# Batch 0 of a fused attention and maxout kernel: DMA work reordered, score pairs ended earlier, more filler matmuls

## The chip, the cores and the metric

The kernel runs on one core of a Trainium2 chip. The metric is the device time of one execution in microseconds (us), and the figure given is the median of several runs. A core has TensorE (PE in the profile; PEld is its loading of weights), VectorE (DVE), ScalarE (ACT) and GpSimd (POOL). SP does no arithmetic: here it issues DMA transfers, and so does POOL. Each of them works through its own list of instructions in order and waits for the others through semaphores. Matmuls write to PSUM, a small memory of eight banks for each partition; everything else lies in SBUF.

## The reference

```python
# attention without softmax: batch 8, seq S = 3072, width D = 256, d_qk = 64
scores = (1 / S) * z @ z.T              # per batch, 3072 x 3072, symmetric
attn   = np.maximum(scores, 0) ** 2
x      = u * (attn @ v)                 # then flattened to 24576 tokens x 256
# maxout layer: d_ff = 1024
h1 = x @ w1
h2 = x @ w2
out = np.maximum(h1, h2) @ w_out        # 24576 x 256, float32
```

The scores are symmetric, so a block of them below the diagonal is the transpose of one above it. The maximum is rewritten as max(h1, h2) = relu(x (w1 - w2)) + x w2, so that the second layer is relu(x w15) w_out + x W2o with w15 = w1 - w2 and W2o = w2 w_out, which are made once on the chip.

## The kernel before

**Tiles and groups.** A batch has 24 tiles of 128 positions. A group is four query tiles (512 positions); six groups make a batch and 48 the whole, in the order of the list `groups`, whose index is i. A group and a key tile are written (g, n) below, of batch 0 unless another is named, and a block (g, blk) is the four key tiles of `blk` against the queries of group g.

**Scores.** `score_pair` (line 125) takes two key tiles against the group's 512 queries: two matmuls (line 134) into two PSUM banks, a Relu of each into `r_sb` (line 149 on ScalarE, or line 145 on VectorE where `dve_half` says so), and one VectorE multiply (line 153) that squares both into `a_sb`. Two pairs fill a block. Only blocks on and above the diagonal are computed, 42 pairs in a batch. Of a block above it, SP issues a DMA transpose (line 157) that makes the mirrored block `at_sb`, which a later group reads. `a_sb` blocks rotate through ten buffers (`apool`), mirrored blocks through thirteen (`tpool`), and the first three loads of z, w1, w2 and w2T take buffers of that same `tpool`: the eleventh mirrored block gets the buffer of w1, the twelfth that of w2, and the thirteenth that of w2T, once these have been read.

**Attention.** `attn_unit` (line 164) does one key tile: four matmuls (line 175) of 64 rows by 512 columns, into the accumulators acc0 and acc1. These take four banks and exist once, so the next group can start only when `drain` (line 179) has emptied them: two ScalarE copies (line 183) and two VectorE adds (line 186). `gate` (line 189) multiplies the sum by u into `xT`; `ff1` (line 202) and `ff2` (line 220) are the maxout layer. From the third group on (i = 2) `ff1` of an earlier group stands between a group's last key tile and the next group's first, so that TensorE has work while the accumulators drain. i = 2 does two of them. The other four PSUM banks (`mm_psum`) rotate among scores, z transposes, `ff1` and `ff2`.

**The order by hand.** The schedule is written out in the main loop (lines 314 to 396); nothing reorders it. `ahead(k)` (line 264) emits score pairs up to the k-th. In groups 0 and 1 of batch 0 one pair is emitted at each even key tile; later one at every third key tile before 22, never more than `AHEAD` = 11 pairs beyond what is needed. Three pairs are done before the loop. z of batch 0 comes in as float32 in three loads and is cast and doubled by `double_first`; its transposes run on TensorE (`zT_pe`, line 96) and are copied to `zT` by ScalarE or VectorE. Later batches use a DMA transpose (`zT_dma`, line 93). Five matmuls on a tile of zeros (line 299) come before all this.

**The queues.** POOL issues the loads of v, u, z and the weights; it runs ahead of the loop, and is held only by a free buffer or, for the weights, by a small VectorE memset into the target (lines 333, 341 and 347) that ties a load to a place in VectorE's list. SP issues the mirrored blocks, the turning of u (`turn_u`, line 115, a DMA transpose), `zT_dma` and the output stores, in order.

Of the kernel before, what the change touches and what calls it, by code (L numbers as in the profile page):

```python
# [11 lines left out]
def kernel(  # L12
# [10 lines left out]
    nc = tc.nc  # L23
# [22 lines left out]
    znat = ctx.enter_context(tc.tile_pool(name="znat", bufs=1))  # L46
    zpool = ctx.enter_context(tc.tile_pool(name="zpool", bufs=2))
    vpool = ctx.enter_context(tc.tile_pool(name="vpool", bufs=2))
    unat = ctx.enter_context(tc.tile_pool(name="unat", bufs=3))
    upool = ctx.enter_context(tc.tile_pool(name="upool", bufs=4))  # L50
    apool = ctx.enter_context(tc.tile_pool(name="apool", bufs=10))
    tpool = ctx.enter_context(tc.tile_pool(name="tpool", bufs=13))
    rpool = ctx.enter_context(tc.tile_pool(name="rpool", bufs=3))
    hpool = ctx.enter_context(tc.tile_pool(name="hpool", bufs=2))
# [66 lines left out]


    A = {}

    def score_pair(b, g, m, dve_half=None, halves=False):
        blk = m // 2
        if m % 2 == 0:
            A[b, g, blk] = apool.tile([P, G, GW], bf16, name="a_sb")
        a = A[b, g, blk]
        s_ps = []  # L130
        for h in range(2):
            rows = ds(h * R, R)
            s_ps.append(mm_psum.tile([P, GW], fp32, name="s_ps", tag="mm"))
            nc.tensor.matmul(  # L134
                s_ps[h],
                zT[b][rows, 2 * m + h, :],
                zT[b][rows, ds(g * G, G), :].rearrange("p t c -> p (t c)"),
                start=True,
                stop=True,
            )  # L140
        r = rpool.tile([P, 2, GW], bf16, name="r_sb")
        k = 2 * (m % 2)
        for h in range(2):
            if h == dve_half:
                nc.vector.tensor_single_scalar(  # L145
                    out=r[:, h, :], in_=s_ps[h], scalar=0.0, op=ALU.max
                )
            else:
                nc.scalar.activation(r[:, h, :], s_ps[h], AF.Relu)  # L149
            if halves:  # L150
                nc.vector.tensor_mul(a[:, k + h, :], r[:, h, :], r[:, h, :])  # L151
        if not halves:
            nc.vector.tensor_mul(a[:, k : k + 2, :], r, r)  # L153
        if m % 2 == 1 and blk > g:

            t = tpool.tile([P, G, G, P], bf16, name="at_sb")
            nc.sync.dma_start_transpose(
                t.rearrange("p k j r -> p (k j) r"), a.rearrange("p k q -> p (k q)")
            )
            A[b, blk, g] = t  # L160

# [100 lines left out]
    def ahead(upto):  # L264
        nonlocal done
        while done < min(upto, len(pairs)):
            early = done < 22
            score_pair(
                *pairs[done],
                dve_half=1 if early and done % 2 == 0 else None,  # L270
                halves=done == 0,
            )
            done += 1
# [6 lines left out]
    with tc.manual_schedule():  # L280
        z32a = first_z(0, 4)
        z32b = first_z(4, 8)
        z32c = first_z(12, 12)
        warm = consts.tile([P, GW], bf16)
        nc.vector.memset(warm, 0.0)
        load_v(0, 0, G)
        make_identity(nc, ident)
        for g in range(1, NG):
            load_v(0, g * G, G)
        load_u(0, 0)  # L290
        load_u(0, 1)
        w1_sb = tpool.tile([P, KD, Dff], bf16, name="w1", tag="at_sb")
        w2_sb = tpool.tile([P, KD, Dff], bf16, name="w2", tag="at_sb")
        w2T_sb = tpool.tile([P, KD, KF, P], bf16, name="w2T", tag="at_sb")


        w_ps = mm_psum.tile([P, GW], fp32, name="warm_ps", tag="mm")
        for k in range(5):
            nc.tensor.matmul(w_ps, warm[:, :P], warm, start=True, stop=True)  # L299

        double_first(z32a, 0, 4)
        zT_pe(0, 0, 4, "dve")
        double_first(z32b, 4, 4)
        double_first(z32b, 8, 4, at=4)
        on_pool = (nc.gpsimd.tensor_copy, nc.gpsimd.tensor_copy)
        for c in range(0, 12, 4):
            double_first(z32c, 12 + c, 4, at=c, copies=on_pool)
        ahead(1)
        zT_pe(0, 4, 4, "dve")
        zT_pe(0, 8, 4, "dve")  # L310
        ahead(3)

        waiting, sums = [], None
        for i, (b, g) in enumerate(groups):
            acc = [
                acc_psum.tile([P, KD, GW], fp32, name=f"acc{half}") for half in range(2)
            ]
            for n in range(NT):
                k = need[i, n]
                if b == 0 and g < 2:  # L320
                    ahead(max(k, done + 1) if n % 2 == 0 else k)
                else:
                    more = n % 3 == 0 and n < 22
                    ahead(max(k, min(done + 1, k + AHEAD)) if more else k)
                if i == 0 and n in (3, 7, 11):
                    zT_pe(0, 9 + n, 4, "act" if n == 7 else "dve")
                attn_unit(b, g, n, acc, n == 0, n == NT - 1)
                if i and n == 4:
                    waiting.append((*groups[i - 1], gate(*groups[i - 1], sums)))
                if i == 0:  # L330

                    if n == 4:
                        nc.vector.memset(w2_sb[:, 0, 0:1], 0.0)
                        nc.gpsimd.dma_start(
                            out=w2_sb, in_=moe_w2.rearrange("(c p) f -> p c f", p=P)
                        )
                    if n == 6:
                        turn_u(0, 0)
                    if n == 14:
                        turn_u(0, 1)  # L340
                        nc.vector.memset(w1_sb[:, 0, 0:1], 0.0)
                        nc.gpsimd.dma_start(
                            out=w1_sb, in_=moe_w1.rearrange("(c p) f -> p c f", p=P)
                        )
                elif i == 1:
                    if n == 2:
                        nc.vector.memset(w_out_sb[:, 0, 0:1], 0.0)
                        nc.gpsimd.dma_start(
                            out=w_out_sb,
                            in_=moe_w_out.rearrange("(c p) d -> p c d", p=P),  # L350
                        )
                        load_u(0, 2)
                    if n == 12:
                        load_u(0, 3)
                elif n == 1 and i + 2 < len(groups):
                    load_u(*groups[i + 2])
                if n == 20 and 0 < i < len(groups) - 1:
                    turn_u(*groups[i + 1])
                if i == 2 and n == 5:
                    nc.vector.tensor_sub(w15_sb, w1_sb, w2_sb)  # L360
                if b + 1 < B:
                    if g == 1 and n == 16:
                        load_z(b + 1, 0, NT)
                    if g == 2 and n == 14:
                        double_z(b + 1, 0, NT)
                        zT_dma(b + 1)
                    if g >= 2 and n in (8, 14)[: 2 if g > 3 else 1]:
                        load_v(b + 1, (g - 2 if n == 8 else g) * G, G)
            if i == 1:
                for dc in range(KD):  # L370
                    tp = mm_psum.tile([P, KF, P], bf16, name="tpw", tag="mm")
                    for j in range(KF):
                        nc.tensor.transpose(tp[:, j, :], w2_sb[:, dc, ts(j, P)], ident)
                    nc.scalar.copy(w2T_sb[:, dc, :, :], tp)
            elif i == 2:
                for dc in range(KD):
                    ps = mm_psum.tile([P, D], fp32, name="w2o_ps", tag="mm")
                    for nb in range(KF):
                        nc.tensor.matmul(  # L379
                            ps,  # L380
                            w2T_sb[:, dc, nb, :],
                            w_out_sb[:, nb, :],
                            start=(nb == 0),
                            stop=(nb == KF - 1),
                        )
                    nc.scalar.copy(W2o_sb[:, dc, :], ps)

            now = waiting if i >= 2 else []
            g_sbs = [ff(w) for w in now[:1]]
            sums = drain(acc)  # L390
            for j, w in enumerate(now):
                if j:
                    g_sbs.append(ff(w))
                ff2(*w, g_sbs[j])
            if now:
                waiting = []
        w = (*groups[-1], gate(*groups[-1], sums))
        ff2(*w, ff(w), last=True)
# [29 lines left out]
```

## Time and profile before

| | us |
|---|---|
| median of 9 runs | 988.6 (986.46 to 989.13) |
| the profiled execution | 987.01 |
| its span, first to last instruction | 985.2 |
| TensorE busy | 971.9 (99% of the span), 8029 matmuls |
| VectorE busy | 497.3 (50%) |
| ScalarE busy | 577.9 (59%) |
| mean granted clock of TensorE, share of full | 0.992 |
| DMA moved | 137.70 MB, 140 GB/s over the span |

A row of the timeline gives the start, the length, the engine and line, the operation with what it writes and reads, and in brackets the idle time of the engine before it with what ended it. "x8" merges eight instructions. The windows view gives, for each stretch, its length, each engine's busy time and number of instructions, then the share of the full TensorE clock that was granted, the busy share of the DMA engines (above 1 where packets overlap) and the rate in GB/s.

### The profile page before, as it was taken

How to read it: one execution, taken by the hardware profiler on the slowest of the kernel's cores; microseconds unless marked ns; L12 is line 12 of the kernel's file. 1: busy time of each engine (PE TensorE's matmuls, PEld its weight loads, DVE VectorE, ACT ScalarE, POOL GpSimd, SP SyncE). 2: the span in 40 equal slices, each digit the busy share in tenths (PEclk: the TensorE clock that was granted, in tenths of full speed). 3: DMA queues.
4: the chain of work that ended last, by engine and by line, in shares of the span. 5: the costliest groups of instructions: out<-in, count | busy, mean ns of one | idle time of the engine just before them, and what ended most of it. 6: DMA issues, size and time to landing. Idle time of an engine off the chain costs nothing.

```text
span 985.2 us, 19196 instructions
## 1 busy us (share of the span) xinstructions
PE 971.9 (99%) x8029; PEld 517.8 (53%) x8029; DVE 497.3 (50%) x759; ACT 577.9 (59%) x1054; POOL 60.4 (6%) x118
## 2 busy tenths in 40 slices
PE   8799999999999999999999999999999999999998
PEld 3355555555555555555555555555555555555555
DVE  7645445645455535555454544455535554455523
ACT  6656546665566646666466664666646665466623
POOL 3100000010000000000000000000000000000000
PEclk9889999999999999999999999999999999999999
DMA  9999668976688766997767957779667895576411
GB/s 191 180 186 187 136 127 151 163 147 128 111 165 164 149 118 130 154 171 130 126 137 153 179 114 141 139 141 169 131 124 136 154 171 116 117 140 128 90 55 43
DMA packets 346006, 137.70 MB, mean 140 GB/s; under 512 B 324544, under 2 KB 325696, under 8 KB 345920
## 3 DMA queue, kind: packets, MB, share of 16 engines
q1 hardware_dynamic: 329504, 106.98, 54.2%
q0 software_dynamic: 16416, 29.50, 20.0%
q8 instruction: 63, 1.03, 0.4%
q14 instruction: 23, 0.19, 0.1%
HBM read 59.77 MB, written 25.17 MB: 86 GB/s over the span
## 4 chain that ended last, share of the span: by engine, by line
PE 97%; DMA 1%; DVE 1%; ACT 0%; issue 0%; DVEq 0%; ACTq 0%
PE acc L175 50%; PE d_ps L206 17%; PE o_ps L235 17%; PE s_ps L134 8%; PE o_ps L227 4%; DMA at_sb<-a_sb 1%; DVE a_sb L153 0%; ACT r_sb L149 0%; PE warm_ps L299 0%; PE w2o_ps L379 0%; DVE r_sb L145 0%; DVE h_sb L186 0%; PE tpz L99 0%; DVE zT L103 0%; DVE a_sb L151 0%
## 5 line engine op out<-in xcount | busy, mean ns | idle before, releaser
L149 ACT ACTIVATE r_sb<-s_ps 128x512 bf16<-128x512 f32 x661 | 359.6, 596 | 178.3 <-PE s_ps L134 178.2
L153 DVE TENSOR_TENSOR a_sb<-r_sb 128x1024 bf16<-128x1024 bf16 x335 | 231.6, 692 | 395.6 <-ACT r_sb L149 394.5
L175 PEld LDWEIGHTS <-v_sb 64*128 64x128 bf16 x4608 | 227.2, 95 | 277.4 <-issue 11.9
L175 PE MATMUL acc<-a_sb,v_sb 64*128 64x512 bf16 x2688 | 332.7, 377 | 0.0
L175 PE MATMUL acc<-at_sb,v_sb 64*128 64x512 bf16 x1920 | 231.6, 381 | 7.0 <-DVE h_sb L186 5.4
L235 PE MATMUL o_ps<-w_out_sb,g_sb 128*128 128x256 bf16 x1536 | 199.1, 273 | 0.0
L206 PE MATMUL d_ps<-xT,w_sb 128*128 128x512 bf16 x768 | 174.1, 380 | 0.0
L216 DVE TENSOR_SCALAR g_sb<-d_ps 128x512 bf16<-128x512 f32 x192 | 132.8, 691 | 77.3 <-PE d_ps L206 77.3
L214 ACT ACTIVATE g_sb<-d_ps 128x512 bf16<-128x512 f32 x192 | 114.7, 598 | 91.3 <-PE d_ps L206 91.3
L235 PEld LDWEIGHTS <-g_sb 128*128 128x128 bf16 x1536 | 150.2, 98 | 20.7
L134 PE MATMUL s_ps<-zT 64*128 64x512 bf16 x672 | 132.0, 383 | 1.1 <-DVE zT L103 0.9
L242 ACT COPY o_sb<-o_ps 128x512 f32<-128x512 f32 x96 | 56.3, 586 | 129.0 <-PE o_ps L235 127.9
L206 PEld LDWEIGHTS <-w_sb 128*128 128x128 bf16 x768 | 71.5, 98 | 98.5 <-issue 19.1
L113 POOL DMA_DIRECT2D un<-in_u_dram x48 | 25.6, 535 | 811.4 <-DMA uT<-un 792.9
L227 PE MATMUL o_ps<-W2o_sb,xT 128*128 128x256 bf16 x384 | 73.3, 273 | 0.0
L186 DVE TENSOR_TENSOR h_sb<-h_sb,acc 128x512 f32<-128x512 f32 x96 | 61.6, 684 | 2.3 <-ACT h_sb L183 2.3
L192 DVE SCALAR_TENSOR_TENSOR xT<-h_sb,uT 128x512 bf16<-128x512 f32 x96 | 61.7, 684 | 0.0
L134 PEld LDWEIGHTS <-zT 64*128 64x128 bf16 x672 | 33.7, 95 | 47.1 <-issue 10.7
L183 ACT COPY h_sb<-acc 128x512 f32<-128x512 f32 x96 | 51.4, 592 | 0.3 <-PE acc L175 0.3
L227 PEld LDWEIGHTS <-xT 128*128 128x128 bf16 x384 | 37.6, 98 | 14.0
L109 POOL DMA_DIRECT2D v_sb<-in_v_dram x48 | 25.9, 546 | 0.8 <-POOLq L412 0.8
L145 DVE TENSOR_SCALAR r_sb<-s_ps 128x512 bf16<-128x512 f32 x11 | 7.5, 683 | 0.8 <-PE s_ps L134 0.8
(33 smaller groups left out, 40.7 us busy)
## 6 DMA issues: line engine op xcount, KB each, us to landing
out_dram<-o_sb SPq DMA_DIRECT2D x47, 512.0 KB, 2.9
v_sb<-in_v_dram POOLq DMA_DIRECT2D x48, 256.0 KB, 6.2
un<-in_u_dram POOLq DMA_DIRECT2D x48, 256.0 KB, 4.4
zn<-in_z_dram POOLq DMA_DIRECT2D x7, 384.0 KB, 5.8
at_sb<-a_sb SPq DMA_TRANSPOSE x120, 4.4
w<-in_moe_w_dram POOLq DMA_DIRECT2D x2, 512.0 KB, 6.9
uT<-un SPq DMA_TRANSPOSE x48, 3.6
w_out_sb<-in_moe_w_out_dram POOLq DMA_DIRECT2D x1, 512.0 KB, 10.2
```

The source lines that it names most:

```text
L134: nc.tensor.matmul(s_ps[h], zT[b][rows, 2 * m + h, :], zT[b][rows, ds(g * G, G), :].rearrange("p t c -> p (t c)"), start=True, stop=True,)
L149: nc.scalar.activation(r[:, h, :], s_ps[h], AF.Relu)
L153: nc.vector.tensor_mul(a[:, k : k + 2, :], r, r)
L175: nc.tensor.matmul(o, v_sb[b][rows, t, ts(dc, P)], mv, start=first, stop=last)
L186: nc.vector.tensor_add(hs[dc], hs[dc], acc[0][:, dc, :])
L192: nc.vector.scalar_tensor_tensor(out=xT[:, dc, :].rearrange("p (t r) -> p t r", r=P), in0=hs[dc].rearrange("p (t r) -> p t r", r=P), scala ...
L206: nc.tensor.matmul(d_ps, w15_sb[:, kc, ts(nb, P)], xT[:, kc, :], start=(kc == 0), stop=(kc == KD - 1),)
L214: nc.scalar.activation(g_sb[:, nb, :], d_ps, AF.Relu)
L216: nc.vector.tensor_single_scalar(out=g_sb[:, nb, :], in_=d_ps, scalar=0.0, op=ALU.max)
L227: nc.tensor.matmul(o_ps[:, t, :], xT[:, dc, ts(t0 + t, P)], W2o_sb[:, dc, :], start=(dc == 0), stop=False,)
L235: nc.tensor.matmul(o_ps[:, t, :], g_sb[:, nb, ts(t0 + t, P)], w_out_sb[:, nb, :], start=False, stop=(nb == KF - 1),)
L242: nc.scalar.copy(o_sb[:, t0 : t0 + 2, :], o_ps)
```

## The change

Buffers: `unat` goes from three to two, `apool` from ten to eleven. Mirroring becomes a function of its own; for groups 0 and 1 of batch 0, blocks 3 to 5 are put on a list `later` and mirrored one at every fourth key tile, from key tile 16 of group 1 on. In the start, filler matmuls of 512 and 128 columns are put between the first steps; they write the first accumulator instead of a bank of `mm_psum`. The z transposes go in larger pieces, copied by ScalarE. Of the first 22 pairs, VectorE takes one Relu in pairs 0 and 1 and in every third, instead of every second. Score pairs are emitted at key tiles 0, 3, 6, 9, 12, 15, 18 and 20 (in groups 0 and 1 of batch 0 at even tiles up to 20). The gate of the previous group moves from key tile 4 to 12. w2 and w1 are loaded at (0, 20), w_out at (1, 10); u of the next group at tile 1 and turned at tile 16; z of the next batch is loaded at (2, 10), and doubled and transposed at (3, 4); v of batch 1 comes at the places in `V_LATE`. The transposes of w2 move from the end of group 1 to key tile 16 of group 2, together with w15.

```diff
@@ -46,9 +46,9 @@
     znat = ctx.enter_context(tc.tile_pool(name="znat", bufs=1))
     zpool = ctx.enter_context(tc.tile_pool(name="zpool", bufs=2))
     vpool = ctx.enter_context(tc.tile_pool(name="vpool", bufs=2))
-    unat = ctx.enter_context(tc.tile_pool(name="unat", bufs=3))
+    unat = ctx.enter_context(tc.tile_pool(name="unat", bufs=2))
     upool = ctx.enter_context(tc.tile_pool(name="upool", bufs=4))
-    apool = ctx.enter_context(tc.tile_pool(name="apool", bufs=10))
+    apool = ctx.enter_context(tc.tile_pool(name="apool", bufs=11))
     tpool = ctx.enter_context(tc.tile_pool(name="tpool", bufs=13))
     rpool = ctx.enter_context(tc.tile_pool(name="rpool", bufs=3))
     hpool = ctx.enter_context(tc.tile_pool(name="hpool", bufs=2))
@@ -121,6 +121,8 @@
 
 
     A = {}
+    later = []
+    V_LATE = [(3, 14), (4, 8), (4, 14), (5, 2), (5, 8), (5, 14)]
 
     def score_pair(b, g, m, dve_half=None, halves=False):
         blk = m // 2
@@ -152,12 +154,19 @@
         if not halves:
             nc.vector.tensor_mul(a[:, k : k + 2, :], r, r)
         if m % 2 == 1 and blk > g:
-
-            t = tpool.tile([P, G, G, P], bf16, name="at_sb")
-            nc.sync.dma_start_transpose(
-                t.rearrange("p k j r -> p (k j) r"), a.rearrange("p k q -> p (k q)")
-            )
-            A[b, blk, g] = t
+            if b == 0 and g < 2 and blk > 2:
+                later.append((b, g, blk))
+            else:
+                mirror(b, g, blk)
+
+    def mirror(b, g, blk):
+
+        t = tpool.tile([P, G, G, P], bf16, name="at_sb")
+        nc.sync.dma_start_transpose(
+            t.rearrange("p k j r -> p (k j) r"),
+            A[b, g, blk].rearrange("p k q -> p (k q)"),
+        )
+        A[b, blk, g] = t
 
 
 
@@ -267,7 +276,7 @@
             early = done < 22
             score_pair(
                 *pairs[done],
-                dve_half=1 if early and done % 2 == 0 else None,
+                dve_half=1 if early and (done % 3 == 0 or done < 2) else None,
                 halves=done == 0,
             )
             done += 1
@@ -294,85 +303,90 @@
         w2T_sb = tpool.tile([P, KD, KF, P], bf16, name="w2T", tag="at_sb")
 
 
-        w_ps = mm_psum.tile([P, GW], fp32, name="warm_ps", tag="mm")
-        for k in range(5):
-            nc.tensor.matmul(w_ps, warm[:, :P], warm, start=True, stop=True)
-
+        def new_acc():
+            return [
+                acc_psum.tile([P, KD, GW], fp32, name=f"acc{half}") for half in range(2)
+            ]
+
+        first_acc = new_acc()
+
+        def keep_warm(cols):
+            for w in cols:
+                nc.tensor.matmul(
+                    first_acc[0][:, 0, :w], warm[:, :P], warm[:, :w], start=True, stop=True
+                )
+
+        keep_warm([GW] * 5 + [P] * 2)
         double_first(z32a, 0, 4)
         zT_pe(0, 0, 4, "dve")
+        keep_warm([P] * 5)
         double_first(z32b, 4, 4)
         double_first(z32b, 8, 4, at=4)
         on_pool = (nc.gpsimd.tensor_copy, nc.gpsimd.tensor_copy)
         for c in range(0, 12, 4):
             double_first(z32c, 12 + c, 4, at=c, copies=on_pool)
         ahead(1)
-        zT_pe(0, 4, 4, "dve")
-        zT_pe(0, 8, 4, "dve")
+        zT_pe(0, 4, 8, "act")
+        keep_warm([P] * 2)
+        ahead(2)
+        keep_warm([P] * 4)
         ahead(3)
 
         waiting, sums = [], None
         for i, (b, g) in enumerate(groups):
-            acc = [
-                acc_psum.tile([P, KD, GW], fp32, name=f"acc{half}") for half in range(2)
-            ]
+            acc = new_acc() if i else first_acc
             for n in range(NT):
                 k = need[i, n]
                 if b == 0 and g < 2:
-                    ahead(max(k, done + 1) if n % 2 == 0 else k)
+                    ahead(max(k, done + 1) if n % 2 == 0 and n < 22 else k)
                 else:
-                    more = n % 3 == 0 and n < 22
+                    more = n in (0, 3, 6, 9, 12, 15, 18, 20)
                     ahead(max(k, min(done + 1, k + AHEAD)) if more else k)
-                if i == 0 and n in (3, 7, 11):
-                    zT_pe(0, 9 + n, 4, "act" if n == 7 else "dve")
+                if i == 0 and n == 5:
+                    zT_pe(0, 12, 8, "act")
+                if i == 0 and n == 11:
+                    zT_pe(0, 20, 4, "act")
                 attn_unit(b, g, n, acc, n == 0, n == NT - 1)
-                if i and n == 4:
+                if i and n == 12:
                     waiting.append((*groups[i - 1], gate(*groups[i - 1], sums)))
-                if i == 0:
-
-                    if n == 4:
-                        nc.vector.memset(w2_sb[:, 0, 0:1], 0.0)
+                if i == 0 and n == 14:
+                    turn_u(0, 0)
+                if i + 1 < len(groups):
+                    if i and n == 1:
+                        load_u(*groups[i + 1])
+                    if n == 16:
+                        turn_u(*groups[i + 1])
+                if (i, n) in ((0, 20), (1, 10)):
+
+                    w_in = ((w2_sb, moe_w2), (w1_sb, moe_w1)) if i == 0 else ((w_out_sb, moe_w_out),)
+                    nc.vector.memset(w_in[0][0][:, 0, 0:1], 0.0)
+                    for w_sb, w in w_in:
                         nc.gpsimd.dma_start(
-                            out=w2_sb, in_=moe_w2.rearrange("(c p) f -> p c f", p=P)
+                            out=w_sb, in_=w.rearrange("(c p) f -> p c f", p=P)
                         )
-                    if n == 6:
-                        turn_u(0, 0)
-                    if n == 14:
-                        turn_u(0, 1)
-                        nc.vector.memset(w1_sb[:, 0, 0:1], 0.0)
-                        nc.gpsimd.dma_start(
-                            out=w1_sb, in_=moe_w1.rearrange("(c p) f -> p c f", p=P)
-                        )
-                elif i == 1:
-                    if n == 2:
-                        nc.vector.memset(w_out_sb[:, 0, 0:1], 0.0)
-                        nc.gpsimd.dma_start(
-                            out=w_out_sb,
-                            in_=moe_w_out.rearrange("(c p) d -> p c d", p=P),
-                        )
-                        load_u(0, 2)
-                    if n == 12:
-                        load_u(0, 3)
-                elif n == 1 and i + 2 < len(groups):
-                    load_u(*groups[i + 2])
-                if n == 20 and 0 < i < len(groups) - 1:
-                    turn_u(*groups[i + 1])
-                if i == 2 and n == 5:
+                if later and n % 4 == 0 and (i > 1 or i == 1 and n > 12):
+                    mirror(*later.pop(0))
+                if i == 2 and n == 16:
                     nc.vector.tensor_sub(w15_sb, w1_sb, w2_sb)
+                    for dc in range(KD):
+                        tp = mm_psum.tile([P, KF, P], bf16, name="tpw", tag="mm")
+                        for j in range(KF):
+                            nc.tensor.transpose(
+                                tp[:, j, :], w2_sb[:, dc, ts(j, P)], ident
+                            )
+                        nc.scalar.copy(w2T_sb[:, dc, :, :], tp)
                 if b + 1 < B:
-                    if g == 1 and n == 16:
+                    late = int(b == 0)
+                    if (g, n) == (2, 10):
                         load_z(b + 1, 0, NT)
-                    if g == 2 and n == 14:
+                    if (g, n) == (3, 4):
                         double_z(b + 1, 0, NT)
                         zT_dma(b + 1)
-                    if g >= 2 and n in (8, 14)[: 2 if g > 3 else 1]:
-                        load_v(b + 1, (g - 2 if n == 8 else g) * G, G)
-            if i == 1:
-                for dc in range(KD):
-                    tp = mm_psum.tile([P, KF, P], bf16, name="tpw", tag="mm")
-                    for j in range(KF):
-                        nc.tensor.transpose(tp[:, j, :], w2_sb[:, dc, ts(j, P)], ident)
-                    nc.scalar.copy(w2T_sb[:, dc, :, :], tp)
-            elif i == 2:
+                    if g >= 3 and n in (8, 14) and not late:
+                        load_v(b + 1, (2 * (g - 3) + (n == 14)) * G, G)
+                    if late and (g, n) in V_LATE:
+                        load_v(1, V_LATE.index((g, n)) * G, G)
+            if i == 2:
                 for dc in range(KD):
                     ps = mm_psum.tile([P, D], fp32, name="w2o_ps", tag="mm")
                     for nb in range(KF):
```

## The prediction

> **What bounds the kernel.** I read the busy shares first, then the granted clock, then windows cut where the clock changes, then TensorE's timeline in them.
>
> ```profile
> PE 971.9 (99%) x8029; PEld 517.8 (53%) x8029; DVE 497.3 (50%) x759; ACT 577.9 (59%) x1054; POOL 60.4 (6%) x118
> PEclk9889999999999999999999999999999999999999
> ```
>
> TensorE is the bound everywhere, and ScalarE and VectorE are half idle on average. But the first slices have a lower clock. The windows (engine columns: busy us and instructions; then granted clock, DMA share, GB/s) say where:
>
> ```profile
> 24.26:27.67 3.41, 1.08 (x12) 0.56 (x11) 2.82 (x5) 1.93 (x4) 0.00 (x0) 1.00 1.14 194
> 27.67:31.09 3.42, 3.42 (x18) 1.49 (x16) 1.40 (x3) 1.58 (x3) 1.27 (x2) 0.50 1.22 247
> 31.09:44.74 13.65, 11.71 (x112) 6.12 (x108) 9.32 (x15) 11.48 (x21) 1.24 (x3) 1.00 1.16 149
> 44.74:48.15 3.41, 2.24 (x12) 0.85 (x14) 1.80 (x3) 1.27 (x3) 1.06 (x2) 0.50 1.22 220
> 48.15:51.57 3.42, 1.81 (x12) 0.49 (x10) 1.34 (x3) 1.08 (x2) 0.00 (x0) 0.50 1.12 152
> 51.57:54.98 3.41, 3.41 (x18) 1.41 (x19) 1.69 (x3) 1.09 (x2) 0.00 (x0) 0.50 1.18 246
> 54.98:65.17 10.19, 10.19 (x95) 5.80 (x92) 5.00 (x8) 5.80 (x11) 0.25 (x1) 1.00 1.20 197
> 470.00:590.00 120.00, 120.00 (x1004) 63.88 (x1002) 60.89 (x93) 72.76 (x134) 6.90 (x13) 1.00 0.77 142
> ```
>
> From 55 us on TensorE is busy without a gap at full clock. In 470 to 590 us key tiles follow each other every 0.432 us (four 512-column matmuls, two row halves at once) and score pairs take 0.216 us; the only irregular steps are some 0.1 us where 64-row and 128-row weights change places, twice a group, and no edit removes them. So the change can only win before 65 us. There the clock halves for one step of 3.41 us after the first gap and three steps after the second, always at multiples of 3.41 us. The gaps, in TensorE's timeline (start, us, work, idle before it and what ended it):
>
> ```profile
> 26.63 1.04 PE L175 MATMUL acc<-at_sb,v_sb 64*128 64x512 bf16 x8 [2.33 <-DVE h_sb L186]
> ...
> 41.41 1.07 PE L373 MATMUL tpw<-ident,w 128*128 128x128 bf16 x16
> ...
> 45.91 2.74 PE L175 MATMUL acc<-at_sb,v_sb 64*128 64x512 bf16 x12 [3.10 <-DVE h_sb L186]
> ...
> 51.53 1.89 PE L175 MATMUL acc<-at_sb,v_sb 64*128 64x512 bf16 x8 [1.61 <-DMA at_sb<-a_sb]
> ```
>
> Groups 0 and 1 have no feed-forward behind which the accumulators can drain, hence the first two gaps. The third is a mirrored block that came late. The chain of waits names it, and the timeline shows what lengthens the second gap:
>
> ```profile
> 43.37 8.12 DMA at_sb<-a_sb
> ```
> ```profile
> 42.12 1.93 ACT L374 COPY w2T<-tpw 128x1024 bf16<-128x1024 bf16 x2 [0.56 <-issue]
> ...
> 43.93 1.09 ACT L183 COPY h_sb<-acc 128x512 f32<-128x512 f32 x2
> 44.56 1.29 DVE L186 TENSOR_TENSOR h_sb<-h_sb,acc 128x512 f32<-128x512 f32 x2 [2.28 <-ACT h_sb L183]
> ```
>
> The drain's two copies stand behind two w2T copies of 1.0 us on ScalarE.
>
> **The change part by part**, in time of TensorE, to the first w2o matmul at 63.25 us.
>
> *Start and group 0 (ends 24.3).* Five fillers of 512 columns stay, thirteen of 128 are added: at the half-clock spacing of the transposes beside them (0.107 us) 1.4 us, laid into waits for casts and zT copies (3.65 to 4.49, 5.86 to 6.84 and 7.3 to 7.6 us are such). Two stand ahead of the first transposes and delay them 0.2 us; that is not covered. The fillers write an accumulator, so one score bank comes free: score pair 2 no longer waits for two VectorE copies (7.58, 7.91). I get attention from about 8.25 instead of 8.46: -0.2. Matmul spacing is still 0.427 us until 10.6, then 0.216 (the clock column, which says 1.00, has no record that early). Steps of 3.41 us counted back from 27.67 end at 10.6 and 7.2. The step to 7.2 was about a third idle; filled to some 90% it should open the clock at 7.2: half of 8.25 to 10.6, -1.1. Here the Trainium skill speaks against it: TensorE: Matmul & The Clock Gate, Part 4, says transposes do not count as busy in the usual way. Twelve transposes (1.3 us) lie in that step; if they count as idle, -1.1 becomes 0. No row here separates the two; I take the gain because the fillers surround them. One score pair fewer before the group's end: -0.2. New cost: at key tile 5 one ScalarE copy of eight transposed tiles (nearest row: w2T's shape, 1014 ns), needed by the pair one tile later, where before VectorE had three tiles' time for four. Behind pair 5's two Relus (0.6 each) it ends about 1.2 us after TensorE wants it: +1.2, minus the 0.5 of small stalls it replaces. Nothing at all would be its price if ScalarE were idle, 2.2 if the next relus queue up too. Moving Relus to ScalarE leaves VectorE 0.69 x 11 + 0.68 x 4 = 10.3 us and ScalarE 12.4 us in a group of about 14: both fit, ScalarE barely. Sum: **-0.8**.
>
> *First gap.* With no pair at tile 22 VectorE reaches the adds when ScalarE's copies allow: 0.1 + 0.6 + two adds of 0.6 and 0.1 to 0.3 of leftover Relu, 2.1 us from last attention matmul to the next, 0.2 of it a score pair: idle 1.9 instead of 2.33: **-0.4**.
>
> *Clock after the gap.* The Trainium skill (same page, Why this matters for your kernels) asks for no idle gap above about 3 us; by that rule 2.33 us costs nothing and 1.9 less. The row says otherwise: 2.33 us idle inside 24.26 to 27.67 halved the next step. So I go by the row: 1.9 us halves the clock only if it falls mostly inside one step, about half the phases: 0.9 us expected, against 1.7 before. By the rule both new gaps would be free and the sum 1.8 better.
>
> *Group 1 (14.8 us).* -0.8 by clock, -0.2 for one pair fewer, -0.3 of small stalls: **-1.3**.
>
> *Second gap (4.5 us with the 1.07 of transposes).* These move to tile 16 of group 2, where two w2T copies (2.0 us) on ScalarE hide behind five key tiles; the drain starts at once: 2.1 us: **-2.4**.
>
> *Group 2 (17.3 us).* +1.3 for the transposes and two weight changes. The 1.6 us wait for the mirrored block goes if block (1,2) lands in time. Mirrors of groups 0 and 1 for blocks 3 to 5 leave SP's queue (six transposes; (0,3), (0,4), (0,5) stood ahead of (1,2)). It would be issued at about 29 us and land by 33 to 40, needed at about 43. Clock: half speed over 45.9 to 55.0 cost 3.8; expected now 0.9. Sum **-3.3**.
>
> *Owed.* 33 instead of 35 pairs done by then: **+0.4**. Pairs stay 11 ahead afterwards and the number of slots per group is unchanged, so later groups neither gain nor lose; ending at tile 20 instead of 21 removes nothing, as ff1 never waited.
>
> *Moved DMA work.* w2 and w1 (6.9 us median to land) are asked for at about 22 us, w_out at 31, all before tile 16 of group 2 (about 49). POOL's queue is in order: u2, u3 and z of batch 1 stand behind the weights' memsets, not urgent. With two u buffers a load still has a group. zT of batch 1 is issued at (3,4), needed at (4,0): 20 tiles, score pairs and 7.9 us of feed-forward, 18 us, against 5.7 to land; the same margin holds in each batch. One wait is added on SP: block (2,5) takes w1's buffer at (2,12), free after w1-w2 at (2,16), about 3 us; behind it stand block (1,5), u's turn and stores, none needed before group 4. All that costs 0 while this cover holds.
>
> Total -0.8 -0.4 -1.3 -2.4 -3.3 +0.4 = **-7.8**. The profiled execution took 987.0 (span 985.2 and 1.8 around it): 979.2. The median of the runs is 1.6 higher, about one more half-clock step (1.7). My sum already holds an average phase, so I add half of it: **980.0**.
>
> **Rivals.**
> 1. *As summed* (66%), 977.5 to 983.0: no halving (-1.8) to both halved, cold start and the longest copy stall (+3).
> 2. *The clock stays down longer* (17%). Each short gap costs two or three steps, as the second did, because the key-tile-5 stall or ScalarE's load leaves every step partly idle: about 5 us back, 985.0. For: a step with 1.2 us idle (44.74) did not open it. Against: nothing then idles within a group.
> 3. *The mirrors are still late* (11%): the DMA share is above 1 until 65 us, and deferring moves bytes, it removes none. Waiting at (2,4) and in the a_sb ring gives 5 to 9 us back: 985 to 988.
> 4. *Slower* (6%), one mechanism: a deferred block keeps its a_sb buffer. The pair at (2,20) writes the buffer of (0,5), whose mirror is issued behind (2,3) at about 42. VectorE's multiply waits in order, behind it the drain adds and its half of ff1's Relus, and TensorE stops. Slack is to about 57 us; from a landing at 67 on nothing is gained, at 72 it is about 993. One transpose of before took 15.5 us (32.00 to 47.53); two like it in a row would do it. But then four transposes later averaged 3 us.
>
> Under 0.2% (2 us) this kernel's measurement tells nothing from no change. Faster: 1 and 2, and half of 3, 88%; same 6%; slower 6%. The range 977.0 to 985.5 holds case 1 and half of case 2.
>
> **What would show it.** TensorE's idle before the first tile of groups 1 and 2 near 1.9 us, released by h_sb; no release by at_sb; at most two half-clock steps; the attention spacing 0.216 from about 7.2 to 8.3 us; a wait of about 1 us for zT near 12 us; first w2o matmul near 55. Wrong if groups 3 to 5 of batch 0 show TensorE waiting for at_sb or VectorE for a buffer, or if batches 1 to 7 take other than 119.4 us each (470.96 to 590.39, ff1 to ff1).

## The result and the profile after

The changed kernel takes 978.16 us (median of 10 runs, nine of them 977.8 to 978.4), against 988.6 in the runs shown and 987.62 over all runs of the kernel before that had been made by then. The ratio is 0.9904, with a 95% interval of 0.9893 to 0.9915. The profiled executions give spans of 976.1 and 985.2 us, so 9.1 us are to be explained.

The page of the changed kernel, busy shares and granted clock:

```profile
PE 966.0 (99%) x8042; PEld 517.2 (53%) x8042; DVE 495.5 (51%) x752; ACT 580.3 (59%) x1058; POOL 61.4 (6%) x118
PEclk9999999999999999999999999999999999999999
```

The early dips of the clock are gone. TensorE's timeline of the changed kernel shows the same seams as before (start, us, work, idle before it and its releaser):

```profile
12.91 0.39 PE L136 MATMUL s_ps<-zT 64*128 64x512 bf16 x2 [0.57 <-ACT zT L103]
...
22.86 0.38 PE L136 MATMUL s_ps<-zT 64*128 64x512 bf16 x2
25.02 1.04 PE L184 MATMUL acc<-at_sb,v_sb 64*128 64x512 bf16 x8 [1.78 <-DVE h_sb L195]
...
38.17 0.57 PE L136 MATMUL s_ps<-zT 64*128 64x512 bf16 x2
40.53 1.47 PE L184 MATMUL acc<-at_sb,v_sb 64*128 64x512 bf16 x12 [1.78 <-DVE h_sb L195]
...
49.05 1.07 PE L374 MATMUL tpw<-ident,w 128*128 128x128 bf16 x16
...
53.72 1.92 PE L393 MATMUL w2o_ps<-w_out_sb,w2T 128*128 128x256 bf16 x16
```

The gaps in front of groups 1 and 2 are both 1.78 us. There is no wait for `at_sb` any more, and the w2o matmuls begin at 53.72 us instead of 63.25. That is 9.5 us earlier; two score pairs are still owed then (0.4), which leaves the 9.1. Cut at the clock's steps of 3.41 us, the windows of the changed kernel are (engine columns: busy us and instructions; then granted clock, DMA share, GB/s):

```profile
3.52:6.93 3.41, 3.41 (x26) 2.09 (x24) 1.84 (x5) 1.96 (x4) 2.70 (x5) 1.00 1.02 219
20.58:23.99 3.41, 2.66 (x26) 1.07 (x22) 2.70 (x6) 2.28 (x5) 0.53 (x1) 1.00 1.09 217
23.99:27.41 3.42, 2.39 (x23) 1.26 (x24) 2.65 (x5) 1.77 (x5) 1.44 (x3) 1.00 0.64 114
37.65:41.06 3.41, 1.63 (x17) 0.62 (x13) 2.37 (x4) 2.16 (x5) 0.00 (x0) 1.00 1.31 185
41.06:44.47 3.41, 3.41 (x36) 1.51 (x34) 0.99 (x2) 1.80 (x4) 0.00 (x0) 1.00 1.22 185
```

The clock of 1.00 in the first row is no reading: the trace's clock records begin at 6.93 us, and up to there 128-column matmuls are 0.107 us apart, against 0.056 behind it, so TensorE ran at half clock.

The first gap is cut by a step's border. The second lies whole in the step from 37.65, which holds 1.78 us idle, and the next step is still at full clock. What this is worth is in the experiments.

### The profile page after: what moved, and what is told of

Same layout as the page of the kernel before. It is cut to its first block, busy times and chain, and to the rows that moved or that the text cites. A ratio compares the mean times of both kernels' runs of the same rounds, so it can differ in the third digit from the quotient of the medians.

```text
span 976.1 us, 19145 instructions
## 1 busy us (share of the span) xinstructions
PE 966.0 (99%) x8042; PEld 517.2 (53%) x8042; DVE 495.5 (51%) x752; ACT 580.3 (59%) x1058; POOL 61.4 (6%) x118
## 4 chain that ended last, share of the span: by engine, by line
PE 98%; DVE 1%; ACT 0%; issue 0%
PE acc L184 51%; PE d_ps L215 17%; PE o_ps L244 17%; PE s_ps L136 8%; PE o_ps L236 4%; PE acc L315 0%; DVE h_sb L195 0%; PE w2o_ps L393 0%; DVE r_sb L147 0%; PE tpz L99 0%; DVE xT L201 0%; ACT r_sb L151 0%; ACT h_sb L192 0%; ACT zT L103 0%; PE tpw L374 0%
## 5 line engine op out<-in xcount | busy, mean ns | idle before, releaser
L184 PE MATMUL acc<-at_sb,v_sb 64*128 64x512 bf16 x1920 | 227.5, 376 | 3.6 <-DVE h_sb L195 3.6
L136 PE MATMUL s_ps<-zT 64*128 64x512 bf16 x672 | 129.7, 379 | 1.4 <-DVE r_sb L147 0.8
L91 DVE COPY zd<-zn 128x1536 bf16<-128x1536 bf16 x14 | 7.1, 552 | 0.0
```

The source lines that it names most:

```text
L136: nc.tensor.matmul(s_ps[h], zT[b][rows, 2 * m + h, :], zT[b][rows, ds(g * G, G), :].rearrange("p t c -> p (t c)"), start=True, stop=True,)
L184: nc.tensor.matmul(o, v_sb[b][rows, t, ts(dc, P)], mv, start=first, stop=last)
```

## Experiments

The same kernels were timed beside the kernel before, whose median was 988.4 to 989.0 in these sessions; the changed kernel's 978.16 is the other reference. Lines of the diffs are against the changed kernel, except for the two that start from the kernel before.

**Small fillers out.** Only the five 512-column fillers stay.

```diff
-        keep_warm([GW] * 5 + [P] * 2)
+        keep_warm([GW] * 5)
...
-        keep_warm([P] * 5)
...
-        keep_warm([P] * 2)
...
-        keep_warm([P] * 4)
```

> The changed kernel (978.2 us) with only the five fillers of 512 columns kept; the thirteen of 128 columns are taken out. My theory: the small fillers make one 3.41 us clock step busy that was a third idle before, so without them the matmul spacing stays 0.427 us until about 10.4 us instead of 7, and attention loses half of 8.2 to 10.4: +1.1 us, 979.3, less 0.2 for the first transposes starting earlier. Rival (small matmuls and transposes do not count for the clock, or the free score bank is what moved the start): no change of the spacing's switch, 978.0 to 978.2.

Measured: 979.87 us (979.24 to 982.37), +1.7. Windows of this run:

```profile
4.08:7.49 3.41, 1.45 (x12) 0.65 (x12) 1.88 (x5) 2.15 (x5) 2.08 (x4) 1.00 1.02 220
7.49:10.90 3.41, 2.81 (x14) 1.09 (x16) 3.27 (x6) 2.24 (x5) 3.02 (x6) 0.50 1.11 203
```

The five large fillers opened the clock already at 4.08 us here, and the step after it, busy for 1.45 of 3.41 us, closed it again for one step. Not all of the +1.7 is the clock's: in this execution the second load of z also landed later (5.30 us against 4.51), and attention starts 0.8 us later (9.08 against 8.29); the half-clock matmuls from there to 10.90 add about 0.9. The fastest run is 1.1 above the changed kernel. So the fillers are worth what was summed (1.1) or a little more. They act in a slightly different way from what I assumed: in the changed kernel's profile they fill the step that opens the clock, and here they are missed in the step that has to keep it open.

The step from 3.52 in the changed kernel is full of small matmuls and transposes. That the transposes count, at least in part, can be read from the traces: without its twelve transposes (1.3 us) that step has at most 2.1 us of work, and it opened the clock, while 2.33 us of fillers alone in the step before it (0.10 to 3.52) and 2.24 us of other matmuls in the kernel before (44.74 to 48.15) did not.

**w2T's transposes back ahead of the drain of group 1.**

```diff
-                    for dc in range(KD):
-                        tp = mm_psum.tile([P, KF, P], bf16, name="tpw", tag="mm")
...
+            if i == 1:
+                for dc in range(KD):
+                    tp = mm_psum.tile([P, KF, P], bf16, name="tpw", tag="mm")
...
```

> The changed kernel with the transposes of w2 back at the end of group 1, ahead of the drain. My theory: two ScalarE copies of 1.0 us stand ahead of the drain again, the idle time before group 2 goes from 1.78 to about 3 us, and the clock halves for at least one 3.41 us step after it: +1.3 idle +1.7 clock -0.2 (two weight changes fewer) = 981.0; with two steps 982.7. Rival (the drain's place does not matter, because the mirrored block was what held group 2): 978 to 979.

Measured: 980.92 us, as the theory had it for one step. In this run the gap is 3.1 us, and its windows show the price of the clock:

```profile
40.12:43.53 3.41, 0.73 (x8) 0.38 (x10) 1.88 (x3) 2.79 (x5) 0.00 (x0) 1.00 1.20 179
43.53:46.95 3.42, 3.42 (x20) 1.22 (x18) 0.61 (x2) 1.08 (x2) 1.07 (x2) 0.50 1.21 246
```

**Mirrored blocks at once.**

```diff
-            if b == 0 and g < 2 and blk > 2:
+            if False and blk > 2:
```

> The changed kernel with every mirrored block issued when its pairs are done, as before; weights still late. If the deferred mirrors are what freed block (1,2): TensorE waits for at_sb at key tile 4 of group 2 again, +1.6 us, and with the clock +3.3: 980 to 981.5. Rival (the later loads of w2, w1 and w_out had already freed the DMA engines): (0,3), (0,4), (0,5) take about 3 us each on SP between 15 and 25 us, block (1,2) lands before 42 us and the time is 978.2.

Measured: 994.32 us (ratio to the kernel before 1.0055, 1.0038 to 1.0071). That is 16 us above the changed kernel, and above the kernel before: both of my numbers were far too small. The waits of this run (in total, times, longest):

```profile
PE acc L184 <- DMA at_sb<-a_sb: 11.4, 1, 11.4
PE s_ps L136 <- DVE r_sb L147: 3.6, 3, 2.6
```

SP's queue holds (0,3), (0,4) and (0,5) in front of (1,2), the first two also in front of uT, and the later weight loads now travel while these run. Block (1,2) landed at 56.16 us, needed at about 44.8. The turn of u landed at 35.55, VectorE waited for it in the gate at (1,12), and with that a PSUM bank came late. The clock is at half for three steps, from 49.65 to 59.89 us; two of them pass within the wait and cost nothing, the third follows it. So the rest of the change, the later weights with it, is a loss without the deferred mirrors.

**Weights early again, mirrors deferred.**

```diff
-                if (i, n) in ((0, 20), (1, 10)):
+                if (i, n) in ((0, 4), (0, 14), (1, 2)):
...
+                    w_in = {(0, 4): ((w2_sb, moe_w2),), (0, 14): ((w1_sb, moe_w1),)}.get(
+                        (i, n), ((w_out_sb, moe_w_out),)
+                    )
```

> The changed kernel with the weights loaded where they were before: w2 at (0, 4), w1 at (0, 14), w_out at (1, 2); the mirrors of groups 0 and 1 stay deferred. If the mirrors' place is what counts (theory): block (1,2) is still the third on SP, lands before 42 us, and the time stays 978 to 979. Rival (both deferrals are needed, the DMA engines are the limit and the turns of u and block (1,2) come late when w2, w1 and w_out are in front of them): a wait of VectorE for uT at (1, 12) or of TensorE for at_sb at (2, 4), 2 to 12 us, 980 to 990.

Measured: 986.25 us, 981.58 to 990.17: 8 us above the changed kernel, with a spread of 8.6 us. The rival was right about the size, but not about the block: it was (0,1), the very first mirror, that TensorE waited for, 9.0 us, at the start of group 1. It was issued at 11.01 us and landed at 31.87; the load of w2, issued at 12.55, landed at 30.39. The windows of this run, then those of the changed kernel:

```profile
15.00:20.00 5.00, 5.00 (x50) 2.22 (x48) 3.40 (x7) 4.52 (x10) 0.09 (x1) 1.00 1.27 97
20.00:25.00 5.00, 2.94 (x28) 1.14 (x24) 4.09 (x7) 3.69 (x7) 0.63 (x1) 1.00 1.34 79
```
```profile
15.00:20.00 5.00, 5.00 (x50) 2.19 (x46) 3.37 (x5) 4.52 (x10) 0.00 (x0) 1.00 1.24 157
20.00:25.00 5.00, 3.24 (x30) 1.36 (x27) 3.97 (x7) 3.87 (x8) 1.54 (x3) 1.00 0.90 184
```

With the weights beside the transposes the DMA engines are as busy by their share, and move about half. In the kernel before, w2 went out at 14.46 us and landed at 22.11 with (0,1) at 21.88, and with the mirrors deferred there (further down) it was 14.62 and 21.83, so the overlap does not always cost that much; what decides is left open.

**Score pairs end as before.**

```diff
-                    ahead(max(k, done + 1) if n % 2 == 0 and n < 22 else k)
+                    ahead(max(k, done + 1) if n % 2 == 0 else k)
...
-                    more = n in (0, 3, 6, 9, 12, 15, 18, 20)
+                    more = n in (0, 3, 6, 9, 12, 15, 18, 21)
```

> The changed kernel with the score pairs ending as before: a pair at key tile 22 in groups 0 and 1 of batch 0, and at 21 instead of 20 in all later groups. My theory: only the two early gaps notice; each idle time grows from 1.78 to 2.1 to 2.4 us, 0.2 us of score work moves ahead of each, and what is lost is the clock: one halved step after one or both gaps, 978.4 without, 980.1 with one, 981.8 with two. Rival (the ends ahead of ff1 cost in each of the 45 groups with ff1): 0.1 us times 45, 982.7, and ff1 shows waits.

Measured: 987.02 us, +8.9, beyond everything expected of it. The gaps grow from 1.78 to 2.0 us each, and each now halves the clock of a step, as the theory said; the second:

```profile
39.10:42.51 3.41, 1.41 (x14) 0.50 (x12) 2.95 (x5) 2.97 (x6) 0.14 (x1) 1.00 1.22 174
42.51:45.92 3.41, 3.41 (x18) 1.24 (x16) 0.29 (x1) 1.01 (x2) 0.00 (x0) 0.50 1.09 199
```

Neither number covers the rest. Two more pairs done early bring the first pair of batch 1 from (4,3) to (3,21), and there zT of batch 1 is not there yet. A third half-clock step follows that wait.

```profile
PE s_ps L136 <- DMA zT<-zd: 4.6, 1, 4.6
```

No wait shows up ahead of ff1 in the later groups: the rival is out.

**The same, with zT of the next batch as early as before.**

```diff
-                    if (g, n) == (2, 10):
+                    if (g, n) == (1, 16):
                         load_z(b + 1, 0, NT)
-                    if (g, n) == (3, 4):
+                    if (g, n) == (2, 14):
```

> The changed kernel with pairs at key tiles 22 and 21 again (987.0 in that run), and z of batch 1 loaded at (1, 16), doubled and transposed at (2, 14), as before the change, in every batch. Theory: with two more pairs done by the end of group 1 the first pair of batch 1 moves from (4, 3) to (3, 21), ahead of zT's landing; with the earlier transpose the 4.6 us wait for zT and the half-clock step after it go: 987.0 - 4.6 - 1.7 = 980.7, what is left over 978.2 being the half-clock steps after the two gaps. Rival (SP's queue is so full that the transpose lands no earlier, or it holds up block (1,2) and others): 985 to 988.

Measured: 980.12 us (978.34 to 983.61). zT landed at 75.13 us instead of 89.68 and the wait is gone. The 6.9 us between these two runs are the coupling of two edits that look unrelated. Of the rest, 2 us, one half-clock step after the second gap is seen in the profiled run.

**A longer gap in front of group 2.** The rival here is the 3 us rule that the prediction names. First with one ScalarE copy ahead of the drain:

```diff
+        junk = consts.tile([P, GW], bf16)
...
+            if i == 1:
+                nc.scalar.copy(junk, warm)
             sums = drain(acc)
```

> The changed kernel with one ScalarE copy of 128x512 into a scratch tile (0.3 to 0.6 us) ahead of the drain of group 1, nothing else. In the traces so far a 3.41 us step that held 1.78 us idle was followed by full clock and one that held 2.0 us by half. Theory (the clock goes by the idle share of a step, with the limit between 52% and 59%): the second gap becomes 2.1 to 2.4 us; where it falls inside one step the next is at half clock, +0.5 and +1.7: runs in two clusters, about 978.6 and 980.3, the median depending on the phase. Rival (only idle gaps of about 3 us count): +0.5 in all runs, 978.6, and no half-clock step.

Measured: 978.03 us. The copy ran from 37.44 to 38.06 us, before the last attention matmul was done; the gap stayed 1.78 us and the run says nothing on the question. Then with three copies:

```diff
+            if i == 1:
+                for _ in range(3):
+                    nc.scalar.copy(junk, warm)
```

> The changed kernel with three ScalarE copies of 128x512 into a scratch tile ahead of the drain of group 1. One copy fitted into ScalarE's idle time before the drain and the gap stayed 1.78 us; three end about 0.5 us after the place where the drain would begin, so the gap becomes about 2.3 us, still far below 3 us. Theory (a 3.41 us step more than 52 to 59% idle halves the clock of the next): where the gap lies inside one step +0.5 +1.7 = 980.4, where a step's border cuts it +0.5 = 978.7; both kinds of run. Rival (only idle gaps of about 3 us count): 978.7 in all runs, no half-clock step.

Measured: 979.12, 978.98 and 979.00 us in three runs, 980.57 and 980.40 in two: the two clusters of the theory, 1.4 us apart. The mean clock of each run agrees: 0.998 in the two, 0.999 to 1.000 in the three, and one half-clock step is 1.7 of 977 us, or 0.002. The profiled run is one of the first three. Its gap is 2.66 us, but a step's border cuts it:

```profile
41.47 1.47 PE L184 MATMUL acc<-at_sb,v_sb 64*128 64x512 bf16 x12 [2.66 <-DVE h_sb L195]
```
```profile
36.42:39.83 3.41, 2.39 (x23) 1.01 (x17) 1.63 (x3) 3.05 (x6) 0.00 (x0) 1.00 1.36 199
39.83:43.24 3.41, 1.77 (x18) 0.83 (x20) 1.98 (x3) 1.79 (x5) 0.00 (x0) 1.00 1.14 201
43.24:46.66 3.42, 3.42 (x35) 1.52 (x32) 1.39 (x2) 2.57 (x5) 1.06 (x2) 1.00 1.22 236
```

A gap of 2.66 us keeps the clock here and one of 2.0 us loses it above, so the length of a gap does not decide alone. Among steps that hold one gap and otherwise attention and score matmuls, how busy the step is does: 1.63 of 3.41 us kept the clock, in seven of the traces, and 1.41 lost it. Busy time as the profile models it is no general measure, though: in the next run the step from 4.72 us, busy for 2.17 us with eight transposes and scattered score matmuls and no pause above 0.7 us, lost the clock too.

**One part alone, from the kernel before.** First, the deferred mirrors with the change's numbers of buffers:

```diff
+            if b == 0 and g < 2 and blk > 2:
+                later.append((b, g, blk))
+            else:
+                mirror(b, g, blk)
...
+                if later and n % 4 == 0 and (i > 1 or i == 1 and n > 12):
+                    mirror(*later.pop(0))
```

> The kernel before with one part of the change: mirrors of groups 0 and 1 for blocks 3 to 5 deferred (and the buffer counts of the change). Theory: the wait of 1.6 us for at_sb in group 2 goes, and of three half-clock steps there one or two; both gaps stay 2.3 and 3.1 us and each still costs a step: -1.6 -1.7 to -3.4, so 3.3 to 5.0 below the kernel before, 983.5 to 985.3. Rival (the late mirrors do nothing without the later weights): no more than 1 below it.

Measured: 983.3 us, 5.1 below the kernel before, at the far end of what the theory gave (3.3 to 5.0). TensorE's wait for `at_sb` is gone from the trace, the waits for `h_sb` are unchanged at 5.4 us in total, and one half-clock step is left after the second gap instead of three. Not every gap cost a step, as the theory had it: the first, of 2.33 us, is cut by a step's border in this trace and cost none; another half-clock step stands at the start, at 8.13 us. Second, the moved transposes of w2:

```diff
-            if i == 1:
-                for dc in range(KD):
...
+                if i == 2 and n == 16:
+                    for dc in range(KD):
...
```

> The kernel before with one part of the change: the transposes of w2 at key tile 16 of group 2 instead of the end of group 1. Theory: what ends last there is the mirrored block (1,2), which landed at 51.5 us whatever TensorE did, so the shorter gap only makes TensorE wait longer for it, and the 1.07 us of transposes now come after: 0 to +1.3 against the kernel before, 988.4 to 989.7. Rival (the parts add up): -2.4 +1.3 and half a clock step less, -1.1 to -2.8: 985.6 to 987.3.

Measured: 989.5 us, ratio 1.0002 (0.9989 to 1.0016). The wait moves on, as the theory said, though it lasts longer than the 1.6 us of before, since the block itself landed at 54.07 us. The profiled run is the slowest of the twelve, 991.92 us, so its wait is no median:

```profile
PE acc L175 <- DMA at_sb<-a_sb: 8.4, 1, 8.4
```

Inside the change the same edit is worth 2.8 us; in front of a late block it is worth nothing.

**A version that beats both.** Three edits on the changed kernel: w2's transposes stand behind the drain of group 1, so TensorE does them in the gap; the later z transposes go in fours again; pair 21 has no Relu on VectorE.

```diff
-            early = done < 22
+            early = done < 21
...
-                if i == 0 and n == 5:
-                    zT_pe(0, 12, 8, "act")
-                if i == 0 and n == 11:
-                    zT_pe(0, 20, 4, "act")
+                if i == 0 and n in (3, 7, 11):
+                    zT_pe(0, 9 + n, 4, "dve" if n == 3 else "act")
...
             sums = drain(acc)
+            if i == 1:
+                for dc in range(KD):
+                    tp = mm_psum.tile([P, KF, P], bf16, name="tpw", tag="mm")
...
```

> A version meant to beat both: the changed kernel with (1) the transposes of w2 put behind the drain of group 1 in the program, so that TensorE does them in the gap and ScalarE copies them after the drain, (2) the later z transposes in pieces of four again, the first copied by VectorE at key tile 3, the others by ScalarE at 7 and 11, (3) pair 21 with both Relus on ScalarE. Theory: -1.1 to -1.3 (1.07 us and two weight changes leave the busy part), -0.57 (the wait for zT), -0.46 (the wait for VectorE behind the gate): 976.0. Rival: w2T's copies (2.0 us) behind the drain hold the Relus of the next pairs and TensorE waits for a bank; then (1) gives back up to 1: 977.2.

Measured: 975.71 us (975.50 to 975.91), ratio to the kernel before 0.9855 (0.9811 to 0.9899), and 2.4 us below the changed kernel. Its timeline at the second gap:

```profile
37.40 1.07 PE L400 MATMUL tpw<-ident,w 128*128 128x128 bf16 x16
38.40 0.39 PE L136 MATMUL s_ps<-zT 64*128 64x512 bf16 x2
39.46 1.47 PE L184 MATMUL acc<-at_sb,v_sb 64*128 64x512 bf16 x12 [0.68 <-DVE h_sb L195]
```

The idle time of that gap is 0.68 us, and the wait behind the gate is gone. The wait for zT shrank from 0.57 to 0.38 us; it did not go. The three edits were run only together.

## Why the prediction was right, and where its sum was off

The forecast was 980.0 us in 977.0 to 985.5, the result 978.16. By the steps of the sum, in the profiled executions:

| step | predicted | measured | from the timelines |
|---|---|---|---|
| start and group 0 | -0.8 | -1.06 | score pair after the last tile, 23.92 to 22.86 |
| first gap | -0.4 | -0.55 | 2.71 to 2.16, start to start |
| group 1 | -1.3 | -1.63 | 14.78 to 13.15 |
| second gap | -2.4 | -2.14 | 4.50 to 2.36 |
| group 2 | -3.3 | -4.15 | 17.34 to 13.19 |
| pairs owed | +0.4 | +0.43 | two pairs of 0.216 |
| sum | -7.8 | -9.10 | spans, 985.2 to 976.1 |

The terms that I named for group 2 add up to -3.2, not -3.3.

- *Start.* Attention starts at 8.29 us (8.25 was expected) with matmuls 0.216 us apart, and the clock opens at 6.93 us. The wait for zT at key tile 5 came as named, with 0.57 us idle and not 1.2: the copy ended at 12.86 us, while TensorE itself came later to that place. The run without small fillers puts 1.1 to 1.7 on the start's clock, and the step from 3.52 opened the clock with its transposes, so taking the trace's side against the Trainium skill's line on transposes (TensorE: Matmul & The Clock Gate, Part 4) was right. The step that I called a third idle was busy for 2.65 of 3.41 us by the windows view (3.78 to 7.19), and did not open the clock either.
- *Gaps and clock.* The gaps were expected at 1.9 us idle and are 1.78. The term that was mis-sized is the clock after them: I charged 0.9 us for each, for half of the phases. The runs show that 1.78 us idle does not halve the clock even when it falls whole in a step, so it is 0 for each. That is 1.2 of the missing 1.3 us, 0.3 in group 1 and 0.9 in group 2; in group 1 a wait of 0.46 us, which I had not named, ate part of it: pair 21's Relu on VectorE stands behind the gate that moved to key tile 12. Going by the row and not by the Trainium skill's 3 us (same page, Why this matters for your kernels) was right as a reading, since 2.0 us lost the clock, though the rule's sum, -9.6, would have lain nearer to the -9.1. That both gaps came for nothing was partly luck: they miss the limit by some 0.2 us, and no row that I had read shows where it lies.
- *Median.* Half a clock step was added for the runs' phases. It was not needed: nine of ten runs lie within 0.6 us, and the mean clock is 0.999 or 1.000 in all ten, since no phase trips the limit.
- *Group 2.* Block (1,2) was issued at 27.84 us and landed at 36.93, needed at about 42.5 (key tile 4): the cover held, with 5 us to spare. Undoing it cost 16 us, where my rival 3 had 5 to 9.
- *What I called covered and nearly was not.* For zT of batch 1 I set 18 us against 5.7 to land. SP's queue of the changed kernel shows what I left out, the instructions in front (start, us for which SP is held):

```profile
73.68 6.55 SPq L165 DMA_TRANSPOSE at_sb<-a_sb  x1
80.32 5.06 SPq L94 DMA_TRANSPOSE zT<-zd  x1
```

It landed at 86.91 us for a pair that runs at 92.85: 6 us of slack, not 12. Two pairs more would have used it up, as the run with pairs at 22 shows.
- *Later groups.* TensorE never waits after 60 us, as argued from the steady rhythm; ending pairs at 20 there did nothing. From ff1 to ff1 a batch takes 119.42 us, as before. The rival of slower time by the `a_sb` ring did not occur in the changed kernel, but its first half did in others: VectorE waited for a deferred mirror to land for 4.1 us in the run with large fillers only, and for 7.0 and 7.7 us in the two with pairs at 22. TensorE lost at most 0.12 us by it.

The parts do not add. The later weights need the deferred mirrors (994.3 without them), the deferred mirrors work better with the later weights (986.3 without), and the moved transposes of w2 give nothing alone (989.5). Not run apart are the larger z pieces, the new share of the Relus, the later gate, and the new places of the v and u loads; what each is worth within the rows of the table stays open.

## What to carry to other kernels

Before pricing a shorter stall, ask what ends last behind it: the same edit was worth 2.8 us once the block behind it was early, and nothing while it was late. When a transfer is moved, write down what stands ahead of it in its queue at that time, not the median time to land. Where a bound TensorE has short gaps, the cheapest repair may be to put its own due work into them (0.68 us left of 1.78).

## What the runs showed of the hardware

- The granted clock moves in steps of 3.41 us whose place differs from execution to execution (the first step at full clock began at 4.97, 5.99 and 6.93 us in three runs with the same start). A step with one gap in which TensorE was busy for 1.63 us left the next at full clock, 1.41 us halved it; a gap of 2.66 us across a border left the clock up, one of 2.0 us inside a step brought it down for one step, up to 1.7 us of TensorE's time. More is needed to open it: at half clock 2.65 us of 3.41 did not (kernel before, 3.78 to 7.19), 2.76 did (large fillers only, 0.66 to 4.08).
- While weight loads of 512 KB ran beside DMA transposes, the DMA engines of one run moved 79 to 97 GB/s at a busy share of 1.27 to 1.34, where the changed kernel moved 157 to 184 in the same stretches. A single transpose then held SP for 13.6 us (17.19 to 30.77). The kernel before had a similar overlap without it; the condition stays open.
